# Joining neighbouring VectorE steps in a long-convolution and gated-MLP block

## The chip, the cores and the metric

The kernel runs on one core of a Trainium2 chip. The time is what the device takes for one execution, in microseconds (us); a kernel's time is the median of several executions. Beside the times there is a profile of one execution. It records every instruction on TensorE (PE), its weight loads (PEld), VectorE (DVE), ScalarE (ACT), GpSimd (POOL) and the DMA queue of SyncE (SP). It begins with the first instruction of the program and ends with the last, so its span is a little shorter than the time of the same execution.

## The reference, cut to what matters

```python
mod = (silu(c) @ w_mod).reshape(1, 6, 1, 576)          # sa, ca, ga, sb, cb, gb
h = layernorm(A_q) * (1 + ca) + sa
k_shift[t] = sum(k[t - j] * shift_k[:, j] for j in range(4))      # four taps along the rows
kv = k_shift * v
y  = causal_convolution(kv, ssm_k) + kv * ssm_D        # over 2048 rows, by FFT in float32
x  = A_q + ga * (h * y)
h  = layernorm(x) * (1 + cb) + sb
x  = x + gb * ((silu(h @ w1) * (h @ w3)) @ w2)         # 576 -> 4608 -> 576
```

There are 2048 rows of 576 columns. Inputs and output are bfloat16.

## The kernel before, in words

**The convolution.** It is cut into eight blocks of 256 rows, `s` = 0 to 7, which lie as 128 partitions by two rows of 576. For each block, `kv_rows` (L335) forms kv on VectorE from `kh`, a tile of five shifted rows of k that one DMA fills: a product with tap 0 into `kv` (L345), then for each of three more taps a product into `kvt` (L348) and a sum into `kv` (L349), at last the product with v (L351). `forward` and `forward2` take kv to a spectrum `X` by matmuls (L313, L327); the filter goes the same way to `V`. `pair` (L414) multiplies a spectrum with a filter, 128 by 3456 elements, into `p` (L424) and adds `p` to the accumulator `z` (L426); the first product of a block goes straight to `z` (L419). Block `s` needs s + 1 such pairs. `real_parts` and `inverse` (L557) lead back to rows, `residual` adds them to x, and a layernorm and transposes (`turn_all`, L589, L619) give `h2T`, the left side of the MLP. `p` comes from the pool `prod` and `kv` and `kvt` from `kvp`; each of these tags has one buffer. Older spectra and filters are spilled to memory (`keep_x` L431, `keep_v` L435) and fetched back (L447).

**The MLP.** It works on four row blocks of 512 rows, `r` = 0 to 3. `stream` computes gate and up of one chunk of 128 hidden columns after the other into PSUM (L948, L959), two chunks at a time. `hide` (L963) finishes a chunk: ScalarE writes silu(gate) into `h3` (L967) and copies up into `u` (L969, four buffers), and VectorE multiplies the two in place (L970), 128 by 512 elements. The last row block has `stream_halves` instead (L1009), with the same three steps (L1030, L1032, L1033). `down` (L1042) multiplies `h3` with w2 (L1060) in two halves of 288 columns, over nine steps of four chunks each. Its four accumulators, one for each tile of 128 rows, lie two and two in PSUM tiles; in the last half of the last row block each has a tile of its own (`tail`). At a half's end VectorE multiplies each accumulator with gb (L1077, 128 by 288 from PSUM) and adds it to x (L1078), and SP stores the rows.

**Order.** While row block r streams, the convolution of the two next blocks runs between its chunks: the generator functions yield a cost in microseconds at each step, and `advance` takes as many steps as are due after each chunk. The compiler then orders each engine's queue by what its own model finds ready, and gives out the buffers of a tag in the course of that, so the order in the trace is not the order of the text. Two parts are fixed: in `first_block` (block 0, and the start of block 1) VectorE, ScalarE and TensorE keep the order of the text, and up to the end of the first 24 chunks the SP queue does. In `first_block` a memset of one element of `wm` (L674), put among the steps of `kv_rows(0)`, holds the DMA of the next columns of w_mod (L152) and what SP issues behind it. Weights of the MLP are issued at L899, L900 and L1051.

Of the kernel before, what the change touches and what calls it, by code (L numbers as in the profile page):

```python
# [9 lines left out]
BF16 = mybir.dt.bfloat16  # L10
# [3 lines left out]
ACT = mybir.ActivationFunctionType  # L14

P = 128
S = 2048
D = 576
F = 4608
B = 256  # L20
NBLK = S // B
H = 288
NF = F // P
RB = 512
NRB = S // RB
FC = 4
# [12 lines left out]
def _ap(t, offset, dims):  # L39

    a = t[:]
    return bass.AP(tensor=a.tensor, offset=a.offset + offset, ap=[list(a.ap[0])] + dims)


class _Kernel:
# [289 lines left out]
    def kv_rows(self, s):  # L335

        nc = self.nc
        kh, vt = self.kh, self.vt
        kv = self.kvp.tile([P, 2, D], BF16, name="kv", tag="kv")
        tmp = self.kvp.tile([P, 2, D], BF16, name="kvt", tag="kvt")  # L340

        def tap(j):
            a = self.shk[:, j, :]
            return bass.AP(tensor=a.tensor, offset=a.offset, ap=[list(a.ap[0]), [0, 2], [1, D]])
        nc.vector.tensor_mul(kv[:], kh[:, 3:5, :], tap(0))  # L345
        yield 0.75
        for j in (1, 2, 3):
            nc.vector.tensor_mul(tmp[:], kh[:, 3 - j:5 - j, :], tap(j))  # L348
            nc.vector.tensor_add(kv[:], kv[:], tmp[:])  # L349
            yield 1.5  # L350
        nc.vector.tensor_mul(kv[:], kv[:], vt[:])  # L351
        self.kv = kv
        yield 0.75
# [292 lines left out]
    def first_block(self):  # L646

        nc = self.nc
        since = len(nc.cur_bb.bb.instructions)
        x1 = self.xo[0]  # L650
        self.angles(nc.vector, 1)
        self.whole_turns(1)
        self.waves(1)
        self.shift_taps()
        self.whole_turns(0)

        ps = self.ps()
        nc.tensor.matmul(ps[0:64, 0, 0:5], self.drow[:], self.ident[0:9, 0:9:2], start=True, stop=True)
        nc.tensor.matmul(ps[64:P, 0, 0:4], self.drow[:], self.ident[0:9, 1:9:2], start=True, stop=True)
        nc.scalar.copy(self.dcol[:, 0:4], ps[:, 0, 0:4])  # L660
        nc.scalar.copy(self.dcol[0:64, 4:5], ps[0:64, 0, 4:5])
        tap = self.knat[:, :, 0]
        nc.gpsimd.tensor_add(tap, tap, self.dcol[:])
        self.waves(0)
        self.warm(3, self.h2T[0][:, 0, :])
        sums = [self.small.tile([P, 1], F32, name="l1" + k, tag="sr" + k) for k in "um"]
        self.run_all(self.k_rows(0))
        self.cond_silu()
        self.warm(4, self.h2T[0][:, 0, :])
        rows = self.kv_rows(0)  # L670
        for _ in range(3):
            next(rows)

        nc.vector.memset(self.wm[0:1, 3 * D:3 * D + 1], 0.0)  # L674
        self.load_mod(3, 2)
        self.load_k(1)
        self.run_all(self.w_spectrum(0))
        self.cond()
        self.run_all(rows)
        mean, rstd = self.quick_stats(x1[:, 1, :], "l1")  # L680
        nmr = self.small.tile([P, 1], F32, name="l1nm", tag="nmr1")
        nc.gpsimd.tensor_mul(nmr[:], mean, rstd)
        nc.gpsimd.tensor_single_scalar(nmr[:], nmr[:], -1.0, op=ALU.mult)
        self.run_all(self.x_spectrum(0))
        self.run_all(self.v_block(0))
        self.load_w13(0, 0)
        self.load_kv(1)
        self.load_x(1)
        self.load_w13(1, 1)
        self.load_gb()  # L690
        self.whole_turns(0, True)
        self.waves(0, True)
        X, V = self.X[0], self.V[0]
# [24 lines left out]
        self.normed(0, 0, *st[0])  # L718
        busy = self.shk[:, 0, 0:512]
        self.warm(6, busy)  # L720
        pt = self.turn_split(0)
        self.warm(2, busy)
        self.normed(0, 1, *st[1])
        self.turned_split(pt, 0)
        pt = self.turn_split(1)
        self.warm(3, busy)
        self.turned_split(pt, 1)
        self.accs.pop(0)
        self.hg.pop(0)
        self.start = since  # L730
        return self.in_order(since, [e.engine for e in (nc.vector, nc.scalar, nc.tensor)])[nc.vector.engine]
# [181 lines left out]
    def stream(self, r, jobs, rate, size, finish=False):  # L913
# [5 lines left out]
        nc = self.nc  # L919
        hT = self.h2T[r % 2]  # L920
        items = []
        for job in jobs:
            m = RB // (job[2] - job[1])
            items += [(job, fi, m) for fi in range(0, FC, m)]
        gus, ws = {}, {}
# [37 lines left out]
        def hide(k):  # L963
            (fc, t0, t1, _, _), fi, m = items[k]
            f = fc * FC + fi
            h3 = self.h3[:, f:f + m, t0:t1]
            nc.scalar.activation(h3, gus[k][:, 0, :].rearrange("p (a t) -> p a t", a=m), ACT.Silu)  # L967
            u = self.hp.tile([P, RB], BF16, name="u", tag="u")
            nc.scalar.copy(u[:], gus[k][:, 1, :])  # L969
            nc.vector.tensor_mul(h3, h3, u[:].rearrange("p (a t) -> p a t", a=m))  # L970
            del gus[k]
            self.advance(rate * 2.05)

# [22 lines left out]
    def stream_halves(self, r, jobs):  # L996

        nc = self.nc
        hT = self.h2T[r % 2]
        items = [(job, fi) for job in jobs for fi in range(FC)]  # L1000
        gus, ws = {}, {}
# [25 lines left out]
        def hide(k):  # L1027
            (fc, _, _, _, _), fi = items[k]
            h3 = self.h3[:, fc * FC + fi, :]
            nc.scalar.activation(h3, gus[k][:, 0, :], ACT.Silu)  # L1030
            u = self.hp.tile([P, RB], BF16, name="u", tag="u")
            nc.scalar.copy(u[:], gus.pop(k)[:, 1, :])  # L1032
            nc.vector.tensor_mul(h3, h3, u[:])  # L1033
        begin(0)
        for k in range(len(items)):
            mark = part(k, 0, slice(AHEAD, None))
            begin(k + 1)
            with self.after(mark):
                part(k, 1)
            hide(k)  # L1040

    def down(self, r, rate):  # L1042
        nc = self.nc
        for h in range(2):

            tail = r == NRB - 1 and h == 1
            accs = [self.ps() for _ in range(4 if tail else 2)]
            acc = [accs[t][:, 0, 0:H] if tail else accs[t // 2][:, t % 2, 0:H] for t in range(4)]
            for f0 in range(0, NF, W2C):
# [20 lines left out]
                    for keep, i in leave[2 * h + f0 // (4 * W2C):][0:1]:  # L1070
                        keep(i)
                self.advance(rate * W2C * 4 * 0.126)
            for t in range(4):
                s, cc = 2 * r + t // 2, t % 2
                x1 = self.xo[s]
                g = self.lnp.tile([P, H], BF16, name="og", tag="og", bufs=2)
                nc.vector.tensor_mul(g[:], acc[t], self.gbrow[:, h * H:(h + 1) * H])  # L1077
                nc.vector.tensor_add(x1[:, cc, h * H:(h + 1) * H], x1[:, cc, h * H:(h + 1) * H], g[:])  # L1078
                if r == NRB - 1:
                    rows = self.out[B * s:B * (s + 1), h * H:(h + 1) * H].rearrange("(p c) d -> p c d", c=2)  # L1080
                    nc.sync.dma_start(rows[:, cc, :], x1[:, cc, h * H:(h + 1) * H])
                elif h == 1 and cc == 1:
                    nc.sync.dma_start(self.out[B * s:B * (s + 1), :].rearrange("(p c) d -> p c d", c=2),
                                      x1[:])

    def begin(self, steps, due=0.0):
        self.steps, self.due, self.spent = steps, due, 0.0
# [108 lines left out]
```

## Time and profile before

| what | before |
|---|---|
| median of 5 executions | 521.32 us (519.91 to 523.8) |
| the profiled execution: time, span | 521.21 us, 519.4 us |
| granted TensorE clock, mean | 0.992 |
| instructions | 9194, of them 554 on VectorE |
| moved by DMA | 107.8 MB, 208 GB/s in the mean |

Engine lines give the busy time, its share of the span and the instructions. The rows of slices show the busy share of each fortieth of the span in tenths. A line of a group reads: line, engine, operation, output from inputs, shapes and count, then busy time and the mean duration of one, then the idle time of the engine before them and what ended it. A line of waits reads: who waited for whom, us in total, how often, the longest. A timeline row reads: start, duration, engine, line, operation, and in brackets the idle time before it.

### The profile page before, as it was taken

What the parts mean: (1) busy time and instruction counts of PE and PEld (TensorE: products, weight loads), DVE (VectorE), ACT (ScalarE), POOL (GpSimd) and SP (SyncE); (2) the same over time, 40 slices, a digit from 0 to 9 for tenths busy, and PEclk for the clock granted to TensorE, in tenths of its full rate; (3) what the DMA queues carried; (4) which work ended last, traced back from release to release, by engine and by line L of the source; (5) the groups of instructions that cost most, each with busy time, mean ns of one, the idle gap of its engine ahead of it and who ended that gap; (6) DMA issues with size and microseconds to landing.
All of it is one profiled execution on the core that took longest, in us unless ns stands there. A gap on an engine that the chain in (4) does not pass through costs nothing.

```text
span 519.4 us, 9194 instructions
## 1 busy us (share of the span) xinstructions
PE 497.4 (96%) x3650; PEld 294.7 (57%) x3650; DVE 344.6 (66%) x554; ACT 294.7 (57%) x581; POOL 23.5 (5%) x43
## 2 busy tenths in 40 slices
PE   7999989789989999999899999999999999999996
PEld 3667765357767444344678543433577544444775
DVE  8899898999995364998988996289662212212012
ACT  6668699468343468769427365875806455555000
POOL 3301001000000000000000000000000000000000
PEclk9989999999989999999999999999999999999999
DMA  8947967838978866578989883544455444541462
GB/s 277 326 145 237 300 214 225 267 99 286 322 269 291 283 192 208 176 249 297 261 268 315 319 266 128 192 155 150 145 157 135 141 142 143 173 145 39 122 176 68
DMA packets 102206, 107.80 MB, mean 208 GB/s; under 512 B 5075, under 2 KB 94228, under 8 KB 102164
## 3 DMA queue, kind: packets, MB, share of 16 engines
q1 hardware_dynamic: 102142, 107.21, 65.5%
q8 instruction: 28, 0.46, 0.3%
q14 instruction: 14, 0.11, 0.1%
q10 hardware_dynamic: 22, 0.01, 0.0%
HBM read 96.00 MB, written 11.21 MB: 206 GB/s over the span
## 4 chain that ended last, share of the span: by engine, by line
PE 61%; DVE 22%; ACT 7%; DMA 5%; issue 2%; SPq 2%; POOL 0%; POOLq 0%; ACTq 0%; DVEq 0%
PE ps L948 21%; PE ps L1060 17%; PE ps L1009 14%; DVE p L424 5%; DVE z L426 4%; PE ps L959 3%; ACT junk L454 3%; DVE h L970 2%; DMA knat<-in_A_ssm_k_dram 2%; DVE kv L349 2%; PE ps L327 1%; DMA wst<-in_B_w_dram 1%; DMA V<-Vd 1%; DVE kvt L348 1%; PE ps L313 1%
## 5 line engine op out<-in xcount | busy, mean ns | idle before, releaser
L948 PE MATMUL ps<-h2T,wst 128*128 128x512 bf16 (+1 forms) x1056 | 200.7, 341 | 1.1 <-ACT W L329 0.8
L1060 PE MATMUL ps<-wst,h 128*128 128x288 bf16 x1152 | 147.1, 288 | 4.7 <-DVE og L1077 2.3
L948 PEld LDWEIGHTS <-wst 128*128 128x128 bf16 x1056 | 100.2, 98 | 85.9 <-issue 14.5
L1060 PEld LDWEIGHTS <-h 128*128 128x128 bf16 x1152 | 113.0, 98 | 35.3 <-issue 6.0
L967 ACT ACTIVATE h<-ps 128x512 bf16<-128x512 f32 x108 | 64.8, 600 | 69.2 <-PE ps L959 41.3
L1009 PE MATMUL ps<-h2T,wst 64*128 64x512 bf16 x648 | 70.3, 376 | 0.0
L970 DVE TENSOR_TENSOR h<-h,u 128x512 bf16<-128x512 bf16 x108 | 45.3, 424 | 30.9 <-ACT u L969 30.7
L969 ACT CAST u<-ps 128x512 bf16<-128x512 f32 x108 | 63.2, 585 | 0.0
L424 DVE TENSOR_TENSOR p<-X,V 128x3456 bf16<-128x3456 bf16 x28 | 54.8, 1957 | 2.5 <-DMA X<-Xd 2.3
L426 DVE TENSOR_TENSOR z<-z,p 128x3456 bf16<-128x3456 bf16 x28 | 54.8, 1958 | 0.2
L1009 PEld LDWEIGHTS <-wst 64*128 64x128 bf16 x648 | 31.3, 94 | 38.4 <-DMA wst<-in_B_w_dram 0.4
L1033 DVE TENSOR_TENSOR h<-h,u 128x512 bf16<-128x512 bf16 x36 | 15.3, 425 | 55.2 <-ACT u L1032 55.2
L1030 ACT ACTIVATE h<-ps 128x512 bf16<-128x512 f32 x36 | 21.5, 597 | 36.3 <-PE ps L1009 36.3
L1077 DVE TENSOR_TENSOR og<-ps,gbrow 128x288 bf16<-128x288 f32 x32 | 13.2, 453 | 41.8 <-PE ps L1060 41.8
L454 ACT ACTIVATE junk<-x 128x576 bf16<-128x576 bf16 x54 | 37.0, 686 | 0.5
L959 PE MATMUL ps<-h2T,wst 64*128 64x512 bf16 (+1 forms) x264 | 32.9, 341 | 0.0
L619 ACT ACTIVATE h2T<-ps,sbcol,cbcol 128x256 bf16<-128x256 bf16 x35 | 16.8, 571 | 14.5 <-PE ps L589 14.5
L348 DVE TENSOR_TENSOR kvt<-kh,shk 128x1152 bf16<-128x1152 bf16 x24 | 18.1, 756 | 4.8 <-DMA kh<-in_A_k_dram 4.6
L1032 ACT CAST u<-ps 128x512 bf16<-128x512 f32 x36 | 20.9, 579 | 0.0
L763 ACT CAST y<-ps 128x576 bf16<-128x576 f32 x14 | 8.6, 647 | 20.8 <-PE ps L557 20.8
L959 PEld LDWEIGHTS <-wst 64*128 64x128 bf16 x264 | 8.5, 94 | 21.0 <-issue 20.1
L349 DVE TENSOR_TENSOR kv<-kv,kvt 128x1152 bf16<-128x1152 bf16 x24 | 18.1, 755 | 0.3
(140 smaller groups left out, 389.9 us busy)
## 6 DMA issues: line engine op xcount, KB each, us to landing
wst<-in_B_w_dram SPq DMA_DIRECT2D x80, 512.0 KB, 4.7
wst<-in_B_w_dram SPq DMA_DIRECT2D x72, 288.0 KB, 3.7
X<-Xd SPq DMA_DIRECT2D x8, 864.0 KB, 5.8
Xd<-X SPq DMA_DIRECT2D x6, 864.0 KB, 6.3
wst<-in_B_w_dram SPq DMA_DIRECT2D x80, 64.0 KB, 2.7
kh<-in_A_k_dram SPq DMA_DIRECT2D x7, 720.0 KB, 7.0
Vd<-V SPq DMA_DIRECT2D x4, 864.0 KB, 7.0
V<-Vd SPq DMA_DIRECT2D x4, 864.0 KB, 7.2
```

Of the source, the lines that this page charges most:

```text
L348: nc.vector.tensor_mul(tmp[:], kh[:, 3 - j:5 - j, :], tap(j))
L349: nc.vector.tensor_add(kv[:], kv[:], tmp[:])
L424: nc.vector.tensor_mul(p[:], X[:], V[:])
L426: nc.vector.tensor_add(z[:], z[:], p[:])
L454: self.nc.scalar.activation(junk[:], src[:, i, :], func, scale=scale, accum_out=out[:, col:col + 1])
L948: nc.tensor.matmul(gus[k][:, i, a * n:(a + 1) * n], w[:, 5 * i + ct, (fi + a) * P:(fi + a + 1) * P], hT[:, ct, t0:t1], start=(first and ct ...
L959: nc.tensor.matmul(gus[k][:, i, a * n:(a + 1) * n], w[rows, 4, (fi + a) * P:(fi + a + 1) * P], hT[rows, 4, t0:t1], start=(first and a == 0 ...
L967: nc.scalar.activation(h3, gus[k][:, 0, :].rearrange("p (a t) -> p a t", a=m), ACT.Silu)
L969: nc.scalar.copy(u[:], gus[k][:, 1, :])
L970: nc.vector.tensor_mul(h3, h3, u[:].rearrange("p (a t) -> p a t", a=m))
L1009: nc.tensor.matmul(gus[k][:, i, :], ws[fc][rows, 5 * i + ct if ct < 4 else 4, cols], hT[rows, ct, :], start=swap == 0 and ct == 4, stop=sw ...
L1060: nc.tensor.matmul(acc[t], self.h3[:, f0 + f, t * P:(t + 1) * P], w[:, f, :], start=(f0 + f == 0), stop=(f0 + f == NF - 1))
```

## The change

Three kinds of neighbouring VectorE steps become one instruction each.

- `hide`, in both streams: two chunks share one `u` of twice the size (still four buffers), and one product over 128 by 1024 elements follows the second chunk's copy.
- `kv_rows`: the products with taps 3, 2 and 1 become one instruction of 128 by 3456 elements, the first of the function, written to a tile `p` of the pool `prod`; `kvt` is gone. The product with tap 0, three sums and the product with v follow. The costs that it yields are 2.0 and five times 0.75 where they were 0.75, three times 1.5 and 0.75, and `first_block` takes four steps ahead of the memset in place of three.
- `down`: the two row tiles of one PSUM tile are multiplied and added together, 128 by 576 elements; the last half of the last row block stays as it was, tile by tile. `og` has one buffer of two row tiles, where it had two of one.

```diff
+        p = self.prod.tile([P, 6, D], BF16, name="p", tag="p")
+        nc.vector.tensor_mul(p[:].rearrange("p (j c) d -> p j c d", j=3), _ap(kh, 0, [[D, 3], [D, 2], [1, D]]),
+                             _ap(self.shk, 3 * D, [[-D, 3], [0, 2], [1, D]]))
+        yield 2.0
+        nc.vector.tensor_mul(kv[:], kh[:, 3:5, :], _ap(self.shk, 0, [[0, 2], [1, D]]))
         yield 0.75
-        for j in (1, 2, 3):
-            nc.vector.tensor_mul(tmp[:], kh[:, 3 - j:5 - j, :], tap(j))
-            nc.vector.tensor_add(kv[:], kv[:], tmp[:])
-            yield 1.5
+        for j in range(3):
+            nc.vector.tensor_add(kv[:], kv[:], p[:, 2 * j:2 * j + 2, :])
+            yield 0.75
         nc.vector.tensor_mul(kv[:], kv[:], vt[:])
...
         rows = self.kv_rows(0)
-        for _ in range(3):
+        for _ in range(4):
             next(rows)
...
-            u = self.hp.tile([P, RB], BF16, name="u", tag="u")
-            nc.scalar.copy(u[:], gus[k][:, 1, :])
-            nc.vector.tensor_mul(h3, h3, u[:].rearrange("p (a t) -> p a t", a=m))
+            if k % 2 == 0:
+                self.u = self.hp.tile([P, 2, RB], BF16, name="u", tag="u")
+            nc.scalar.copy(self.u[:, k % 2, :], gus[k][:, 1, :])
+            if k % 2 == 1:
+                h3 = self.h3[:, f - m:f + m, t0:t1]
+                nc.vector.tensor_mul(h3, h3, self.u[:].rearrange("p b (a t) -> p (b a) t", a=m))
...
+                g = self.lnp.tile([P, 2, H], BF16, name="og", tag="og")
+                for cc in ((slice(0, 1), slice(1, 2)) if tail else (slice(0, 2),)):
+                    n = cc.stop - cc.start
+                    ps = acc[2 * a + cc.start].unsqueeze(1) if tail else accs[a][:, :, 0:H]
+                    nc.vector.tensor_mul(g[:, cc, :], ps, _ap(self.gbrow, h * H, [[0, n], [1, H]]))
+                    nc.vector.tensor_add(x1[:, cc, cols], x1[:, cc, cols], g[:, cc, :])
+                    if r == NRB - 1:
+                        nc.sync.dma_start(rows[:, cc, cols], x1[:, cc, cols])
+                    elif h == 1:
+                        nc.sync.dma_start(rows, x1[:])
```

More of the change, by code (lines that the diff above doesn't have):

```diff
@@ L339, in kv_rows @@
         kv = self.kvp.tile([P, 2, D], BF16, name="kv", tag="kv")
[L340 to L345, printed above, removed]
+        p = self.prod.tile([P, 6, D], BF16, name="p", tag="p")
[3 more added lines that the diff above has]
+        nc.vector.tensor_mul(kv[:], kh[:, 3:5, :], _ap(self.shk, 0, [[0, 2], [1, D]]))
         yield 0.75
-        for j in (1, 2, 3):
-            nc.vector.tensor_mul(tmp[:], kh[:, 3 - j:5 - j, :], tap(j))
-            nc.vector.tensor_add(kv[:], kv[:], tmp[:])
-            yield 1.5
+        for j in range(3):
+            nc.vector.tensor_add(kv[:], kv[:], p[:, 2 * j:2 * j + 2, :])
+            yield 0.75
         nc.vector.tensor_mul(kv[:], kv[:], vt[:])
@@ L965, in hide @@
             f = fc * FC + fi
-            h3 = self.h3[:, f:f + m, t0:t1]
-            nc.scalar.activation(h3, gus[k][:, 0, :].rearrange("p (a t) -> p a t", a=m), ACT.Silu)
-            u = self.hp.tile([P, RB], BF16, name="u", tag="u")
-            nc.scalar.copy(u[:], gus[k][:, 1, :])
-            nc.vector.tensor_mul(h3, h3, u[:].rearrange("p (a t) -> p a t", a=m))
+            nc.scalar.activation(self.h3[:, f:f + m, t0:t1], gus[k][:, 0, :].rearrange("p (a t) -> p a t", a=m),
+                                 ACT.Silu)
+            if k % 2 == 0:
[4 more added lines that the diff above has]
+                nc.vector.tensor_mul(h3, h3, self.u[:].rearrange("p b (a t) -> p (b a) t", a=m))
             del gus[k]
@@ L1030, in hide @@
             nc.scalar.activation(h3, gus[k][:, 0, :], ACT.Silu)
-            u = self.hp.tile([P, RB], BF16, name="u", tag="u")
-            nc.scalar.copy(u[:], gus.pop(k)[:, 1, :])
-            nc.vector.tensor_mul(h3, h3, u[:])
+            if k % 2 == 0:
+                self.u = self.hp.tile([P, 2, RB], BF16, name="u", tag="u")
+            nc.scalar.copy(self.u[:, k % 2, :], gus.pop(k)[:, 1, :])
+            if k % 2 == 1:
+                h3 = self.h3[:, fc * FC + fi - 1:fc * FC + fi + 1, :]
+                nc.vector.tensor_mul(h3, h3, self.u[:])
         begin(0)
@@ L1072, in down @@
                 self.advance(rate * W2C * 4 * 0.126)
-            for t in range(4):
-                s, cc = 2 * r + t // 2, t % 2
+            cols = slice(h * H, (h + 1) * H)
+            for a in range(2):
+                s = 2 * r + a
                 x1 = self.xo[s]
[L1076 to L1084, printed above, removed]
+                rows = self.out[B * s:B * (s + 1), :].rearrange("(p c) d -> p c d", c=2)
+                g = self.lnp.tile([P, 2, H], BF16, name="og", tag="og")
[8 more added lines that the diff above has]
+                        nc.sync.dma_start(rows, x1[:])
     def begin(self, steps, due=0.0):
```

## The prediction

> **What bounds the kernel now.** I read the page's busy shares and slices first, then TensorE's waits, the groups by shape, and VectorE's timeline around the waits that bear on it.
>
> ```profile
> PE 497.4 (96%) x3650; PEld 294.7 (57%) x3650; DVE 344.6 (66%) x554; ACT 294.7 (57%) x581; POOL 23.5 (5%) x43
> PE   7999989789989999999899999999999999999996
> DVE  8899898999995364998988996289662212212012
> ```
>
> TensorE has work in 96% of the span, so a faster VectorE can only close TensorE's gaps. VectorE is full in slices 7 to 12 and 17 to 24 (13 us each).
>
> ```profile
> PE ps L557 <- DVE z L543: 2.9, 1, 2.9
> PE ps L1060 <- DVE og L1077: 2.3, 1, 2.3
> PE ps L1060 <- DMA wst<-in_B_w_dram: 1.6, 1, 1.6
> PE ps L378 <- DVE og L1077: 1.0, 1, 1.0
> ```
>
> All of TensorE's gaps sum to 17.8 us; these four, at 100.1, 149.9, 257.4 and 292.2 us, are the ones that hang on VectorE. The third does so indirectly: SP issues the weights behind a spill of X (L431, at 249.43) that waits for VectorE's L365 (ends 249.4).
>
> ```profile
> L424 DVE TENSOR_TENSOR p<-X,V 128x3456 bf16<-128x3456 bf16 x28 | 54.8, 1957 | 2.5 <-DMA X<-Xd 2.3
> L970 DVE TENSOR_TENSOR h<-h,u 128x512 bf16<-128x512 bf16 x108 | 45.3, 424 | 30.9 <-ACT u L969 30.7
> L348 DVE TENSOR_TENSOR kvt<-kh,shk 128x1152 bf16<-128x1152 bf16 x24 | 18.1, 756 | 4.8 <-DMA kh<-in_A_k_dram 4.6
> L1077 DVE TENSOR_TENSOR og<-ps,gbrow 128x288 bf16<-128x288 f32 x32 | 13.2, 453 | 41.8 <-PE ps L1060 41.8
> ```
>
> The last figure ahead of the second bar is the mean ns of one. What an instruction costs its queue is another number, in the timeline's first column (starts):
>
> ```profile
> 91.70 0.42 DVE L970 TENSOR_TENSOR h<-h,u 128x512 bf16<-128x512 bf16 x1
> 92.04 0.75 DVE L531 TENSOR_TENSOR hg<-hg,brow 128x1152 bf16<-128x1152 bf16 x1
> ...
> 135.10 1.96 DVE L424 TENSOR_TENSOR p<-X,V 128x3456 bf16<-128x3456 bf16 x1
> 136.96 0.76 DVE L345 TENSOR_TENSOR kv<-kh,shk 128x1152 bf16<-128x1152 bf16 x1
> 137.63 0.76 DVE L348 TENSOR_TENSOR kvt<-kh,shk 128x1152 bf16<-128x1152 bf16 x1
> 138.43 0.76 DVE L349 TENSOR_TENSOR kv<-kv,kvt 128x1152 bf16<-128x1152 bf16 x1
> ...
> 143.06 1.95 DVE L419 TENSOR_TENSOR z<-X,V 128x3456 bf16<-128x3456 bf16 x1
> 144.93 0.75 DVE L571 TENSOR_TENSOR hg<-hg,y 128x1152 bf16<-128x1152 bf16 x1
> 145.60 1.96 DVE L426 TENSOR_TENSOR z<-z,p 128x3456 bf16<-128x3456 bf16 x1
> ...
> 170.08 0.76 DVE L348 TENSOR_TENSOR kvt<-kh,shk 128x1152 bf16<-128x1152 bf16 x1 [4.60 <-DMA kh<-in_A_k_dram]
> ...
> 193.31 1.95 DVE L424 TENSOR_TENSOR p<-X,V 128x3456 bf16<-128x3456 bf16 x1
> ...
> 208.48 0.76 DVE L345 TENSOR_TENSOR kv<-kh,shk 128x1152 bf16<-128x1152 bf16 x1 [0.20 <-PE ps L327]
> ...
> 209.40 0.75 DVE L349 TENSOR_TENSOR kv<-kv,kvt 128x1152 bf16<-128x1152 bf16 x1
> ```
>
> See three things. The next start comes 0.34 us after a 0.42 us instruction. An instruction that needs the one before it starts later: 137.63 to 138.43 is 0.80, where 136.96 to 137.63 is 0.67. And the compiler's order runs a tap product far ahead of its block: `kvt` is written at 170.08 and read at 209.40.
>
> **The change, part by part.** *Price of an instruction saved.* Durations: (756-424)/640 = 0.519 ns an element, so 424-512x0.519 = 158 ns fixed. Starts (335 ns from an L970 to the next instruction, 667 from an L345, as in the rows at 91.70 and 136.96): (667-335)/640 is the same slope and 335-266 = 69 ns fixed, as neighbours overlap by about 90 ns. Removed: 72 of the 144 `h` products, 2 x 8 in `kv_rows`, 14 + 14 in `down` (the last half, 4 + 4, stays split): 116 of 554. By durations that is 116 x 0.158 = 18.3 us of VectorE, by starts 116 x 0.069 = 8.0. [...]
>
> *silu times up.* Per pair 2 x 0.335 becomes 1024 x 0.519 + 69 = 0.60: 0.07 saved. The first of two products comes one chunk later (about 2 us), and VectorE waits for ACT's `u` once where it did twice. Only `down` reads h3, and the last chunk is finished at the same place as before plus 0.27 us, at least one weight step of 2 us (16 x 0.126) ahead of its use: cost nothing; without that cover 0.27 us a row block. ACT's silu and copies are as before; `u` holds eight chunks where four were held, and no wait for it shows before L969 (idle 0.0).
>
> *kv_rows.* In a chain, 136.96 to 143.06 is 6.10 us; now 1.87 (as L424 to the next start) + 4 x 0.79 + 0.67 = 5.70: 0.40 saved. Interleaved with other work, 8 x 0.668 = 5.34 becomes 1.87 + 5 x 0.668 = 5.21: 0.13. The joined product reads overlapping rows with taps in falling order, which no row shows: at least 0.60 per 1152 as in L424, at most one element a cycle as L1077's slope of 1.04 ns (364 - 64 = 300 ns for 288), 3.6 us. I take the former, since L348 with its repeated tap already costs what L351 does (756, 760). In the first block VectorE ends `kv` at 11.9 in place of 12.3, but X is handed over by ACT at 15.54 and TensorE takes `kv` at 12.45 behind its own work: nothing gained. The memset (L674) that lets SP issue w_mod, knat and weights moves from 9.96 to 10.35; w_mod then lands at 18.5 for a use at 22.4, and the first weights feed L948 at 33: nothing, at most 0.4. The order of SP's and POOL's issues elsewhere is as written before; only `kh` may be released earlier, its load stands in the same place of SP's queue.
>
> *down.* Two products of 0.364 and two sums of 0.217 become 0.67 and 0.37: 1.16 to 1.04. The first result waits for both row tiles (4 x 0.126 = 0.5 us), and PSUM is returned after one product of 0.75 (L564, 576 f32) in place of a second one of 0.45: 0.3 later where VectorE is free. TensorE asks for that bank 8 matmuls (1.0 us) into the next half: covered, 0.2 to spare; else 0.3 a half. One output DMA of two in the second-last half falls away, beside TensorE. In the last half `g` has one buffer: its third product waits for the second sum. Before, sums at 515.42 and 516.12 close the kernel; I count +0.2 (0 to 0.4).
>
> *Sum with the order kept.* In the full stretch 79 to 151.3 lie 24 `h` products (12 x 0.07 = 0.8), one interleaved and one chained `kv_rows` (0.13 + 0.40): 1.3 us, all taken from the 2.3 at 149.9. In row block 1, a wait of 1.6 us for X at 239.5 eats what was saved earlier; behind it 0.3 reaches the gap at 257.4. The 1.0 at 292.2 follows three pair products released by a DMA (280.4): nothing. Row block 3 and TensorE's tail have VectorE idle: nothing. So -1.3 - 0.3 + 0.2 = -1.4. The profiled run took 521.21 (519.4 span + 1.8), the median is 521.32, so no correction: 519.8.
>
> *What the new buffer adds.* `kvt` was private; now the taps sit in `p`, of which there is one, shared with every pair product. The row at 170.08 shows a tap product issued when only kh is there, 38 us before `kv` is free (208.48). If the joined product is placed likewise, `p` stays taken until three sums after 208.5, about 211.5. The pair at 193.31 and its sum (2 x 1.87 = 3.74 us) then move from a stretch where VectorE is half idle (4.9 of 13 us at 196 to 209) into the full one behind it. X's sums at 249.4, the spill, SP's weights and the gap at 257.4 follow: 3.74 less the 0.6 saved there, +3.1. The same stands again at 305.31 (its `kv` at 338.59), with the pair at 313.70: 0 to 3.1 for the inverse at 357, since z has 5 us to spare at 388; I take 1.5. Who waits is thus VectorE's whole queue, behind it TensorE's inverse and SP.
>
> **The rivals.** *1, likeliest: p is held.* -1.3 + 3.1 + 1.5 + 0.2 = +3.5: 524.7 (522.7 to 527.5). For it: 170.08 and 305.31, and a `p` held from 135.10 to 145.60 already. Against: the order is new, and it may give `p` to the pair first. *2, order kept, small gain:* 519.8 (518 to 521). For it: full VectorE ahead of 149.9. Against: it needs the same queue with another buffer. *3, the other side, faster: the held `p` pushes `kv_rows` out of the full stretch.* The 6.1 us at 136.96 wait for the sum at 145.60 and fall behind `og` (151.34), into VectorE's idle time after 157, and the gap at 149.9 closes (2.3). Tap work that goes behind the pairs at 96.05 and 249.62 likewise frees X and z there: the 1.6 at 257.4, and some 0.8 of the 2.9 at 100.1. 521.2 - 4.7 + 0.2 = 516.7. It decides as soon as 2.3 us of work pass `og`. *4, the joined taps run at one element a cycle:* 8 x 1.73 = 13.8 us more VectorE, 3.5 of it before 149.9 and about 1 before 257.4: less 1.6 saved, +3: 524.
>
> **How the numbers follow.** About 0.5% (2.6 us) is what a measurement here can tell from none. Case 1 has 0.42 (0.32 slower, 0.10 within), case 2 0.28 (0.22 within, 0.06 faster), case 3 0.16 (faster), case 4 and other new waits of the reordered queues 0.14 (0.12 slower, 0.02 within). Faster 0.22, same 0.34, slower 0.44. Case 1 gives 524.7; its own range stands above. The range for all reaches from case 3's middle to a bit beyond case 1's end: 516.5 to 528.
>
> **What would show it.** VectorE: 438 instructions, busy near 326 us, but only some 8 us less time from start to start; 690 ns for 128x1024, 1957 for the joined taps. Case 1: a `p` written from kh near 170 and its last sum after 209, no pair between, and a longer gap at 257. Case 2: every pair at its old place, the gap at 149.9 near 1. Case 3: `kv_rows` of block 4 after 151. I am wrong if TensorE's gaps shrink by over 3 us in all, or if the difference lies where VectorE is idle.

## The result, and the profile after

| what | before | changed |
|---|---|---|
| median | 521.42 us (517.95 to 524.85, 79 runs) | 520.62 us (519.03 to 522.37, 44 runs) |
| ratio to before | | 0.998 (95% interval 0.9968 to 0.9993) |
| profiled execution: time, span | 521.21, 519.4 us | 521.62, 519.8 us |
| granted clock, mean | 0.992 | 0.989 |
| VectorE busy, instructions | 344.6 us, 554 | 337.4 us, 438 |
| TensorE idle up to its last matmul | 17.8 us | 14.4 us |

The change brings 0.2%, about 1 us. The interval excludes 1, so the gain is there, but it is small. The busy shares, the slices and the groups of the changed kernel:

```profile
PE 500.7 (96%) x3650; PEld 295.8 (57%) x3650; DVE 337.4 (65%) x438; ACT 293.9 (57%) x581; POOL 23.6 (5%) x43
PE   6999989989999999999997999999999999999996
DVE  8799898998898172998977996189761211211012
L422 DVE TENSOR_TENSOR p<-X,V 128x3456 bf16<-128x3456 bf16 x28 | 54.7, 1955 | 1.8 <-DMA V<-Vd 1.4
L971 DVE TENSOR_TENSOR h<-h,u 128x1024 bf16<-128x1024 bf16 x54 | 37.1, 687 | 22.7 <-ACT u L968 22.7
```

From the groups with shapes apart, the two other joined instructions:

```profile
L341 DVE TENSOR_TENSOR p<-kh,shk 128x3456 bf16<-128x3456 bf16 x8 | 15.6, 1954 | 0.5 <-ACT shk L205 0.4
L1086 DVE TENSOR_TENSOR og<-ps,gbrow 128x576 bf16<-128x576 f32 x14 | 10.6, 756 | 29.2 <-PE ps L1064 28.8
```

Each joined instruction runs at the expected speed; the joined taps are as fast as a pair (1954 ns against 1955). TensorE's waits have changed their names:

```profile
PE ps L587 <- ACT h2row L582: 4.0, 5, 2.2
PE ps L327 <- DVE kv L349: 2.4, 1, 2.4
PE ps L198 <- DMA shk_raw<-in_A_shift_k_dram: 2.2, 1, 2.2
PE ps L376 <- POOL knat L661: 1.3, 1, 1.3
PE ps L1064 <- ACT u L968: 1.0, 1, 1.0
```

The gaps at 100.1 (2.9), 149.9 (2.3), 257.4 (1.6) and 292.2 (1.0) are gone. New are 1.3 us at 6.75 (behind `knat`), 2.4 at 104.8 (behind `kv` of block 3) and 2.2 at 280.2 (behind `h2row`; in it a tile of rows after the second layernorm waits to be transposed). Cut at TensorE's own milestones (the first matmul of each stretch), the two executions compare so:

| stretch, us | before | changed | difference |
|---|---|---|---|
| start to the stream of row block 0 | 33.0 | 33.8 | +0.8 |
| to its down | 94.4 | 93.9 | -0.5 |
| to the stream of row block 1 | 43.2 | 40.5 | -2.7 |
| to its down | 78.2 | 78.9 | +0.7 |
| to the stream of row block 2 | 40.9 | 43.8 | +2.9 |
| to TensorE's end | 225.5 | 224.2 | -1.3 |
| to the span's end | 4.2 | 4.7 | +0.5 |

So little moved in the total because 4.5 us were gained and 4.9 lost in this pair of executions (+0.4 in the profiled times; the medians say -0.8). The experiments take the gains and the losses apart.

**Where block 4's `kv_rows` went.** VectorE's timeline of the changed kernel around 150 us (start, duration, operation):

```profile
146.51 1.95 DVE L422 TENSOR_TENSOR p<-X,V 128x3456 bf16<-128x3456 bf16 x1
148.38 0.75 DVE L1086 TENSOR_TENSOR og<-ps,gbrow 128x576 bf16<-128x576 f32 x1
...
153.11 1.96 DVE L424 TENSOR_TENSOR z<-z,p 128x3456 bf16<-128x3456 bf16 x1
154.98 0.76 DVE L406 TENSOR_TENSOR V<-V 128x1152 bf16<-128x1152 bf16 x1
155.65 1.96 DVE L341 TENSOR_TENSOR p<-kh,shk 128x3456 bf16<-128x3456 bf16 x1
```

The taps come after the pair and after `og`: before, the six microseconds of `kv_rows` lay at 136.96, ahead of it.

**Where the loss at 280 us comes from.** First VectorE, then GpSimd:

```profile
275.18 0.16 DVE L458 TENSOR_TENSOR l2v<-l2s 128x2 f32<-128x2 f32 x1 [0.59 <-ACT junk L452]
276.79 1.96 DVE L422 TENSOR_TENSOR p<-X,V 128x3456 bf16<-128x3456 bf16 x1 [1.45 <-DMA V<-Vd]
278.66 0.15 DVE L460 SCALAR_TENSOR_TENSOR l2v<-l2q,l2v 128x2 f32<-128x2 f32 x1
278.78 1.96 DVE L424 TENSOR_TENSOR z<-z,p 128x3456 bf16<-128x3456 bf16 x1
281.32 0.16 DVE L470 TENSOR_TENSOR l2n<-l2s,l2r 128x2 f32<-128x2 f32 x1 [0.58 <-POOL l2r L464]
```

```profile
278.96 2.32 POOL L464 TENSOR_TENSOR l2r<-l2v,neghalf 128x2 f32<-128x2 f32 x1 [36.37 <-DVE l2v L460]
```

A pair stands in VectorE's queue between the two halves of block 5's second layernorm variance. It waits for a filter from memory (1.45 us) and takes 1.96 us; the power on GpSimd, which needs that variance, then takes 2.32 us beside the sum of 1.96 us. In the kernel before, the variance came first, and the power took 0.69 us:

```profile
278.41 0.16 DVE L460 TENSOR_TENSOR l2v<-l2s 128x2 f32<-128x2 f32 x1
279.22 0.16 DVE L462 SCALAR_TENSOR_TENSOR l2v<-l2q,l2v 128x2 f32<-128x2 f32 x1 [0.65 <-ACT junk L454]
280.25 0.16 DVE L472 TENSOR_TENSOR l2n<-l2s,l2r 128x2 f32<-128x2 f32 x1 [0.87 <-POOL l2r L466]
280.46 1.96 DVE L424 TENSOR_TENSOR p<-X,V 128x3456 bf16<-128x3456 bf16 x1
```

```profile
279.52 0.69 POOL L466 TENSOR_TENSOR l2r<-l2v,neghalf 128x2 f32<-128x2 f32 x1 [33.03 <-DVE l2v L462]
```

The shift (`l2n`), `h2row` and TensorE's transposes follow the power.

### The profile page after: what moved, and what is told of

Its sections match the earlier page's. It is cut to its first block, busy times and chain, and to the rows that moved or that the text cites. A ratio compares the mean times of both kernels' runs of the same rounds, so it can differ in the third digit from the quotient of the medians.

```text
span 519.8 us, 9076 instructions
## 1 busy us (share of the span) xinstructions
PE 500.7 (96%) x3650; PEld 295.8 (57%) x3650; DVE 337.4 (65%) x438; ACT 293.9 (57%) x581; POOL 23.6 (5%) x43
## 4 chain that ended last, share of the span: by engine, by line
PE 66%; DVE 18%; ACT 8%; DMA 3%; issue 2%; POOL 2%; SPq 0%; POOLq 0%; DVEq 0%; ACTq 0%
PE ps L946 20%; PE ps L1064 20%; PE ps L1010 13%; ACT junk L452 3%; PE ps L957 3%; DVE p L422 3%; DVE z L424 2%; PE ps L313 2%; DVE h L971 2%; DVE p L341 2%; DVE kv L347 2%; PE ps L327 2%; PE ps L555 1%; DMA wst<-in_B_w_dram 1%; DMA V<-Vd 1%
## 5 line engine op out<-in xcount | busy, mean ns | idle before, releaser
L422 DVE TENSOR_TENSOR p<-X,V 128x3456 bf16<-128x3456 bf16 x28 | 54.7, 1955 | 1.8 <-DMA V<-Vd 1.4
L424 DVE TENSOR_TENSOR z<-z,p 128x3456 bf16<-128x3456 bf16 x28 | 54.7, 1954 | 0.2
L971 DVE TENSOR_TENSOR h<-h,u 128x1024 bf16<-128x1024 bf16 x54 | 37.1, 687 | 22.7 <-ACT u L968 22.7
L1037 DVE TENSOR_TENSOR h<-h,u 128x1024 bf16<-128x1024 bf16 x18 | 12.5, 692 | 58.1 <-ACT u L1034 58.1
L1086 DVE TENSOR_TENSOR og<-ps,gbrow 128x576 bf16<-128x576 f32 (+1 forms) x18 | 12.3, 689 | 44.1 <-PE ps L1064 43.6
L582 ACT ACTIVATE h2row<-x,l2n,l2r 128x576 bf16<-128x576 bf16 (+1 forms) x24 | 14.0, 663 | 10.5 <-DVE l2n L470 10.5
L347 DVE TENSOR_TENSOR kv<-kv,p 128x1152 bf16<-128x1152 bf16 x24 | 18.1, 756 | 0.3
```

The costliest lines, as they stand in the source:

```text
L347: nc.vector.tensor_add(kv[:], kv[:], p[:, 2 * j:2 * j + 2, :])
L422: nc.vector.tensor_mul(p[:], X[:], V[:])
L424: nc.vector.tensor_add(z[:], z[:], p[:])
L971: nc.vector.tensor_mul(h3, h3, self.u[:].rearrange("p b (a t) -> p (b a) t", a=m))
```

## The experiments

Ratios are to the kernel before, with their 95% intervals; where a difference is given in us, it is that of two ratios times 521.4 us. Most intervals are about 1 us to either side or more, so two rows that differ by less than some 1.5 us (an estimate from the intervals) are not told apart. Two stretches of each profile are set beside them: the start of row block 0's stream, and the time from row block 1's down to row block 2's stream.

| kernel | ratio | idle, us | stream 0 from | down 1 to stream 2 |
|---|---|---|---|---|
| before | 1 | 17.8 | 33.0 | 40.9 |
| changed | 0.998 (0.9968 to 0.9993) | 14.4 | 33.8 | 43.8 |
| p shared, nothing joined | 0.9965 (0.9947 to 0.9983) | 14.2 | 32.0 | 39.2 |
| taps joined alone | 0.9945 (0.9920 to 0.9969) | 13.2 | 34.4 | 40.2 |
| products of down joined alone | 1.0069 (1.0043 to 1.0094) | 19.3 | 33.8 | 42.8 |
| changed, down apart | 0.9916 (0.9896 to 0.9935) | 14.3 | 34.7 | 39.6 |
| changed, down apart, knat on VectorE | 0.9895 (0.9854 to 0.9937) | 13.7 | 32.5 | 39.8 |

**The same kernel again.** A profile is one execution; this one asks which readings belong to the program.

> The changed kernel once more, to see what of its first profile comes back. If the readings describe the program: TensorE idle 14 to 15 us in all, a gap of 2.4 us near 104.8 behind kv, one of 2.2 us near 280.2 behind h2row, no gap over 1 us near 149.9 and 257.4, the sum into knat on GpSimd at 1.6 us, MLP stream of row block 0 from 33.8. If they are accidents of one execution (DMA arrivals): these places and sizes move by a microsecond or more.

Measured: idle 14.8 us, gaps of 2.4 at 104.9 and 1.8 at 279.6, the sum into `knat` again a gap of 1.3 for TensorE, the stream from 33.9. The places stand; a gap of 0.8 at 256.1 is new. Sizes below about 1 us are not to be trusted from one profile.

**The buffer without the joining.**

```diff
-        tmp = self.kvp.tile([P, 2, D], BF16, name="kvt", tag="kvt")
...
         for j in (1, 2, 3):
+            tmp = self.prod.tile([P, 2, D], BF16, name="p", tag="p")
             nc.vector.tensor_mul(tmp[:], kh[:, 3 - j:5 - j, :], tap(j))
```

> The kernel before, with nothing joined; the tap products only take the buffer of the pairs, p, instead of one of their own. Theory A (order): the buffer is given out in the order of the text, so block 4's kv_rows goes behind its pairs by itself, after 150, and the gap at 149.9 (2.3 us) closes with 554 instructions as before; VectorE busy stays near 344 us; TensorE idle falls from 17.8 to about 15; GpSimd's sum into knat stays short and the stream of row block 0 starts at 33.0; time 1 to 2 us under the kernel before. Theory B (fewer instructions give the gain): the gap at 149.9 stays above 1.5 us and the time is that of before or longer.

Theory A holds. With no instruction saved, the ratio is 0.9965 and the gap at 149.9 is gone. The timeline shows the separate products behind the pair and `og`:

```profile
146.43 1.95 DVE L424 TENSOR_TENSOR p<-X,V 128x3456 bf16<-128x3456 bf16 x1
...
155.31 0.75 DVE L348 TENSOR_TENSOR p<-kh,shk 128x1152 bf16<-128x1152 bf16 x1
```

The reason is in how `p` is given out. The text asks for a tile of `p` 36 times; in the changed kernel's trace all 36 writes to `p` come in just that order, though most other instructions do not. For block 4 the text names its pairs with older spectra first, then the taps. A buffer that a tag has only once is handed from user to user in the order of the text, and so the shared tag fixes an order that a private `kvt` had left free.

**The taps alone.** The edit of `kv_rows` and of `first_block` on the kernel before, nothing else.

> The kernel before with only the taps joined (silu times up and the products of down as before). Theory A (order): the gap at 149.9 closes as in the changed kernel, block 4's taps come after 150, and the first block has the same loss (sum into knat 1.6 us, stream of row block 0 from 33.8); time within 0.5 us of the changed kernel, 520 to 521. Theory B (the 72 silu products saved do it): the gap at 149.9 keeps over 1 us and the time is that of before.

0.9945: the gap at 149.9 is closed without 100 of the 116 saved instructions, and the time is about 3 us under before where the changed kernel has 1. It has the first block's loss (a gap of 1.3 at 6.76), but not the one at 280. Theory A is right on the gap and too high on the time: something else in the change costs some 2 us.

**The sum into knat on VectorE.**

```diff
-        nc.gpsimd.tensor_add(tap, tap, self.dcol[:])
+        nc.vector.tensor_add(tap, tap, self.dcol[:])
```

> The changed kernel with one instruction moved: the sum of ssm_D into column 0 of knat runs on VectorE ahead of the joined taps, not on GpSimd beside them. Theory A (GpSimd is held[...]): the transposes of the filter start about 1 us earlier than 8.05, TensorE's gap of 1.3 us at 6.75 shrinks to about 0.3, and the stream of row block 0 starts at 33.0 or before; 0.5 to 1 us under the changed kernel. Theory B (the memset that comes 0.4 us later delays w_mod, and with it the stream): the stream still starts at 33.6 to 33.8, and the time is that of the changed kernel.

In the kernel before, GpSimd's sum of 128x5 elements took 0.25 us. In the changed kernel it takes 1.65, beside VectorE's joined taps (5.96 to 7.92), and TensorE waits for it. Here VectorE does it in 0.18. In this order, before, changed (two rows) and this run (two rows):

```profile
6.79 0.25 POOL L663 TENSOR_TENSOR knat<-knat,dcol 128x5 bf16<-128x5 bf16 x1 [1.53 <-DMA knat<-in_A_ssm_k_dram]
```

```profile
6.35 1.65 POOL L661 TENSOR_TENSOR knat<-knat,dcol 128x5 bf16<-128x5 bf16 x1 [1.09 <-DMA knat<-in_A_ssm_k_dram]
8.05 1.25 PE L376 MATMUL ps<-ident,knat 128*128 128x128 bf16 x10 [1.30 <-POOL knat L661]
```

```profile
6.72 0.18 DVE L661 TENSOR_TENSOR knat<-knat,dcol 128x5 bf16<-128x5 bf16 x1 [1.18 <-DMA knat<-in_A_ssm_k_dram]
6.96 1.25 PE L376 MATMUL ps<-ident,knat 128*128 128x128 bf16 x10 [0.21 <-DVE knat L661]
```

The transposes start at 6.96 (8.05), the gap is 0.21 (1.30), the stream starts at 33.4 (33.8). GpSimd's sum was held beside the taps, as theory A has it; what else the traces show of its condition, two operands in SBUF, stands in the last section. In time, 0.9967 (0.9947 to 0.9987) does not stand clear of the changed kernel's 0.998.

**Block 4's taps ahead of its last pair.**

```diff
                 V = self.old_v(s0 - j, s0)
+                if s0 == 4 and j == 3:
+                    yield from self.kv_rows(s0)
                 yield from self.pair(X, V, s0)
...
-            yield from self.kv_rows(s0)
+            if s0 != 4:
+                yield from self.kv_rows(s0)
```

> The changed kernel with one step moved in the text: kv_rows of block 4 stands ahead of the last pair of its spectra, so that the taps take p before that pair. All instructions stay joined. Theory A (order): the taps are ahead of 151.3 on VectorE again, and if the order is what closed the gap, TensorE waits 1 us or more at 149.9 again (about 1.0 by the prediction's sum for joined instructions in the old order); 0.5 to 1.5 us over the changed kernel. Theory B (instructions saved): no gap over 0.5 us at 149.9 and the time of the changed kernel.

1.0023 (1.0007 to 1.0040), 2.2 us over the changed kernel, yet no gap at 149.9: neither theory said that. The experiment was badly made: at 145.74 the taps (1.95 us) stand where the pair (1.95 us) stood at 146.51, ahead of `og`, and the sums stay behind it. The same length was exchanged, so it does not test what was meant. Why the time grew stays open: the two profiled executions differ by 0.9 us only.

**The variance ahead of the pair.** An order-only dependence on VectorE puts the second sum into block 6 (the pair at 276.79) behind the shift of block 5.

```diff
+        if s == 6 and self.count[s] == 2:
+            self.tc.add_manual_dep(
+                self.newest(), self.l2_last.name,
+                mybir.DependencyInfo(mybir.DependencyClass.NoSync, mybir.DependencyReason.DATA),
+                reason="program order")
```

> The changed kernel with one order fixed on VectorE: the pair that starts at 276.8 goes behind the variance and shift of block 5's second layernorm. Theory A (a pair in front of the variance, and GpSimd's power beside VectorE's sum, hold up h2row): the power takes 0.7 us in place of 2.3, the gaps at 280.2 and 283.1 (2.19 + 0.47) fall below 1 us, the granted clock stays at full in 282 to 286, and row block 2's stream starts at about 288 in place of 290.9; 2 to 4 us under the changed kernel. Theory B (h2row is bound by ACT and by the sums of squares before it): h2row comes at the same time, the gaps stay, no change.

0.9934 (0.9912 to 0.9957), 2.4 us under the changed kernel. The power takes 0.69 us, the gap at 280.2 is gone, row block 2's stream starts at 286.7 (290.9). One pair and one sum moved behind three small instructions bring more than the whole change. Theory A.

**Silu products apart again.** Both `hide` functions as before.

> The changed kernel with the silu products chunk by chunk again (72 more instructions); taps and the products of down stay joined. Theory A (they lie in VectorE's full stretches at 0.07 us a pair, and beside other work elsewhere): VectorE about 5 us more from start to start, the gap at 149.9 at most 0.9 us, time 0 to 1 us over the changed kernel. Theory B (their duration counts, 0.16 us each): 1.5 to 3 us over it.

0.9985 (0.9966 to 1.0005): no difference from the changed kernel can be seen. The 72 instructions, most of those saved, bring nothing that shows; the 0.8 us that the prediction counted for them would lie within the intervals.

**Taps apart again.** `kv_rows` as before, `u` with three buffers for want of space.

> The changed kernel with kv_rows as before (kvt in a buffer of its own, which leaves room for three u tiles of two chunks, not four); silu times up and the products of down stay joined. Theory A (order): the gap at 149.9 is there again, 1.0 to 1.5 us, the one at 104.8 is gone, the first block starts the stream at 33.0; that is case 2 of the prediction: 519.5 to 521. Theory B (the shared p brought nothing): TensorE's idle time as in the changed kernel or less and a time of 519 or less.

1.0133 (1.0100 to 1.0165), far outside what was expected. The old gaps are back (1.49 at 154.2, 1.45 at 259.3), the gap behind `kv` of block 3 is gone and the first block is short (stream from 32.6), as theory A has it. But there are also 4.26 us at 101.9, 1.91 at 41.5 and 2.07 at 285.5 behind `h2row`. The last shows that the loss near 280 does not come with the taps. How much of the rest is due to three `u` tiles is not separated.

**Products of down apart again; and joined alone.** What the runs with the loss at 280 have in common (the changed kernel, and those with silu, taps or knat altered) is the joined `og`.

> The changed kernel with the products of down tile by tile as before; taps and silu products stay joined. The gap behind h2row near 280 is in the three runs with joined og (changed kernel, silu apart, taps apart) and not in the run with joined taps alone. Theory A (the shorter og moves the compiler's order, so that a pair comes ahead of the second layernorm's variance): the variance is ahead of the pairs again, GpSimd's power takes 0.7 us, no gap over 1 us near 280, last out-DMA as before; 2 to 3.5 us under the changed kernel. Theory B (the shared p brings that pair forward): gap and time stay as in the changed kernel.

> The kernel before with only the products of down joined. Theory A (og moves the order at the end of row block 1): a gap of about 2 us behind h2row near 283 and row block 2's stream 2 to 3 us later than in the kernel before, the tail 0.3 longer, the gaps at 149.9 and 257.4 still there; 1 to 3 us over the kernel before. Theory B (as the prediction counted it: 0.12 us saved a half, 0.2 lost at the end): no change.

Apart: 0.9916 (0.9896 to 0.9935), 3.3 us under the changed kernel. Joined alone: 1.0069 (1.0043 to 1.0094), 3.6 us over the kernel before, where 1 to 3 were expected; the gap behind `h2row` is 1.3 us and not 2, and row block 2's stream starts 2.8 us later (292.5 against 289.7). Joined, `og` is a loss, and most of it hangs on an order: the dependence that put the variance ahead of the pair gave 2.4 us of it back. VectorE of the kernel with only `og` joined:

```profile
279.22 0.16 DVE L460 TENSOR_TENSOR l2v<-l2s 128x2 f32<-128x2 f32 x1 [0.54 <-ACT junk L454]
279.90 1.96 DVE L424 TENSOR_TENSOR p<-X,V 128x3456 bf16<-128x3456 bf16 x1 [0.52 <-DMA V<-Vd]
281.78 0.15 DVE L462 SCALAR_TENSOR_TENSOR l2v<-l2q,l2v 128x2 f32<-128x2 f32 x1
```

VectorE and GpSimd of the changed kernel with `og` apart:

```profile
274.17 0.16 DVE L458 TENSOR_TENSOR l2v<-l2s 128x2 f32<-128x2 f32 x1
274.98 0.16 DVE L460 SCALAR_TENSOR_TENSOR l2v<-l2q,l2v 128x2 f32<-128x2 f32 x1 [0.65 <-ACT junk L452]
```

```profile
275.29 0.69 POOL L464 TENSOR_TENSOR l2r<-l2v,neghalf 128x2 f32<-128x2 f32 x1 [33.84 <-DVE l2v L460]
```

With `og` joined, the compiler puts the pair ahead of the second half of the variance, and otherwise behind it, unless the dependence forbids it. Why it does so is open. The joining also took `og` from two buffers to one, and no run has the one without the other. All 17 profiles of this study fall into two groups: the power takes 2.32 or 2.33 us in the nine with joined `og` and no repair, and 0.69 us in the eight others.

**The first block's taps apart.** `kvt` takes the buffer of `y` in block 0.

> The changed kernel with the first block's taps one by one as before (kvt in the buffer of y, which the first block doesn't use); blocks 1 to 7 joined. Theory A (GpSimd's sum into knat waits out the VectorE instruction beside it, 2 us joined, 0.75 apart): the sum takes 0.75 us at most, the transposes start by 7.5, row block 0's stream starts 0.8 to 1.5 us earlier than in the changed kernel (33.8), and the time is lower by as much. Theory B (the start is set by a DMA): no change in either.

The sum takes 0.28 us and the stream starts at 32.7, as theory A says, but the ratio is 0.998 (0.9953 to 1.0006): the time did not fall by the 0.8 to 1.5 us of theory A, as far as this interval tells. Over all profiles, the stream starts at 34.4 in the mean of the eight with the slow sum and at 32.9 in the mean of the nine others, so the 1.5 us at the start are real; that they reach the end is not shown by this run.

**Three repairs together.** The two diffs above, and in the last half `og` of the second tile in the buffer of `y`.

> The changed kernel with three repairs: the sum into knat on VectorE, the pair at 276.8 behind the second layernorm's variance and shift, and in the last half a second buffer (that of y) for og. Theory A (the three losses add): 0.7 + 2.3 + 0.4 us under the changed kernel, about 516.5 to 517.5, TensorE idle near 11 us, span end 4.2 to 4.4 behind TensorE's end. Theory B (a loss repaired early is given back at a later wait): 518 or more.

0.9918 (0.9895 to 0.9942), 3.2 us under the changed kernel, where the three losses sum to 3.4. It cannot be told from the one dependence alone (0.9934), and TensorE's idle time is 14.6 us, not the 11 that theory A said, so this run does not show that the losses add. The span ends 4.2 us behind the last matmul, as in the kernel before (4.7 in the changed one): the single `og` buffer had cost the tail some 0.5.

**A held `p`, built on purpose.**

```diff
         yield from self.mix(self.x_spectrum(s0), beside())
+        if s0 == 4:
+            yield from self.kv_rows(s1)
         yield from self.x_sums(s0)
```

(and not a second time in `others`.)

> The changed kernel with one step moved in the text: kv_rows of block 5 stands ahead of the pair of block 4's new spectrum, so the taps take p early, some 10 us before kv is free, and that pair (at 211 in the changed kernel) has to wait for the third sum. It is what case 1 of the prediction described. Theory A (a held p costs as case 1 said): X's sums and the spill behind them come some 3 us later, a gap of 2 to 5 us at 257 for weights, 2 to 3.5 us over the changed kernel. Theory B (the 3.7 us of pair that wait have slack there, as case 3 said of such moves): block 5's spectrum comes earlier, no new gap over 1 us, within 1 us of the changed kernel.

1.0062 (1.0033 to 1.0091), 4.3 us over the changed kernel. The taps are written at 195.44, 12 us before `kv` is free (207.50), and the pair waits until 215.64 (211.22). That is more than the 2 to 3.5 of theory A, and the place is another: there is no gap at 257. SP issues the fetch of the next filter 3.1 us later than in the changed kernel (273.44 against 270.34), and the pair at 280.14 waits for a filter:

```profile
280.14 1.96 DVE L422 TENSOR_TENSOR p<-X,V 128x3456 bf16<-128x3456 bf16 x1 [3.66 <-DMA V<-Vd]
```

Two pairs now stand ahead of the second half of the variance, `h2row` leaves a gap of 3.7 us, and the granted clock falls to 0.50 behind it (290 to 294).

**Silu joined on top of the shared `p`.**

> The kernel before with the tap products in p (nothing joined there) and the silu products of two chunks joined: what 72 fewer instructions are worth once the order is settled. Theory A (TensorE's remaining gaps behind VectorE are about 4.5 us, and 0.07 us a pair of products is saved): 0 to 1.5 us under the kernel with the shared p alone (0.9965 of the kernel before). Theory B (the later product of the first chunk and one u tile of two chunks cost something): as long as that kernel or longer.

0.9982 (0.9964 to 1.0001), against 0.9965 with the shared `p` alone: no gain, theory B, within what can be told.

**Taps and silu joined, down apart, knat on VectorE.**

> The changed kernel with the products of down tile by tile (as in the version that ran 0.9916 of the kernel before) and, in addition, the sum into knat on VectorE ahead of the taps. Theory A (the first block's loss is a loss of its own): row block 0's stream starts near 33 in place of 34.7, and the time falls 0.7 to 1.5 us further, to about 0.989 to 0.990. Theory B (what starts earlier waits later): 0.9916 again.

0.9895 (0.9854 to 0.9937), 514.78 us in the median: the fastest kernel here, 1.05% under the kernel before and 0.85% under the changed one. The stream starts at 32.5 and idle is 13.7 us. Whether the last 0.2% over the version with `og` apart is real, the intervals leave open.

## Why the prediction was right or wrong, point by point

- **Case 1, "p is held", the likeliest: wrong at its first step.** The row at 170.08 was read as "a tap product is issued when only kh is there". That was true of a private buffer. A tile of a shared tag is given out in the order of the text (36 of 36 writes), and the text names the pairs first. The words before the prediction, that the compiler gives out a tag's buffers in the course of its ordering, had the same error. In the changed kernel, block 5's taps take `p` at 218.25, behind the pairs at 190.91 and 211.22, and no pair waits for them as case 1 had it. The step that failed is the placement; the +3.1 and +1.5 that hung on it did not come. Whether they were sized rightly is not shown: a held `p` built on purpose costs 4.3 us, but not through the gap at 257.
- **Case 3, the pushed `kv_rows`: the mechanism came about.** `kv_rows` of block 4 stands behind `og` at 155.65, and the gaps at 149.9, 257.4 and 100.1 closed. Alone, the shared buffer brings 1.8 us and the joined taps 2.9 us, not 4.7: closing the gap at 100.1 opened one of 2.4 at 104.8, because block 3's taps come behind the same pair.
- **Case 2's number was right by accident.** 519.8 (518 to 521) holds the median of 520.62, but the order was not kept, and the result is a gain of about 4 (the change with `down` apart) and a loss of about 3 (the joined `og`).
- **Price of an instruction.** The shapes came as worked out: 0.60 us from an L971 to the next start, 1.87 for the joined taps, and VectorE's busy time fell by 7.2, close to the 8.0 counted by starts. "Near 326" was a wrong inference: the durations of the groups do add up to some 18 us less (count times mean: 358.3 against 376.6), but the engine's busy line (337.4 against 344.6) counts the overlap of neighbours once. Case 4 took L1077's slope, 1.04 ns an element, for the joined taps (756 ns for L1086's 576 columns against 453 for L1077's 288 give 1.05); they run in 1954 ns, 0.57 an element, which refutes it. Its name, one element a cycle, is the author's: no run shows a cycle of VectorE. For the 72 silu products the sum had 0.8 us in the full stretch; two comparisons show nothing of it, but could not show so little.
- **down: the step that was missed.** "1.16 to 1.04" holds only where the compiler puts another instruction between a product and its sum. Where none stands there, the prediction's own rule for an instruction that needs the one before it applies, 0.79 from start to start in place of 0.67, and the second product comes only after the first sum, which frees the one buffer. First the changed kernel, then the kernel before:

```profile
167.38 0.76 DVE L1086 TENSOR_TENSOR og<-ps,gbrow 128x576 bf16<-128x576 f32 x1 [1.43 <-PE ps L1064]
168.17 0.46 DVE L1087 TENSOR_TENSOR x<-x,og 128x576 bf16<-128x576 bf16 x1
168.73 0.76 DVE L1086 TENSOR_TENSOR og<-ps,gbrow 128x576 bf16<-128x576 f32 x1
```

```profile
170.75 0.82 DVE L1077 TENSOR_TENSOR og<-ps,gbrow 128x288 bf16<-128x288 f32 x2
171.49 0.52 DVE L1078 TENSOR_TENSOR x<-x,og 128x288 bf16<-128x288 bf16 x2
171.92 0.82 DVE L1077 TENSOR_TENSOR og<-ps,gbrow 128x288 bf16<-128x288 f32 x2
```

  From the first product to the third, or to the second joined one, it is 1.35 us where it was 1.17: nothing is saved there. The tail's +0.2 came as +0.5. And the products of down joined alone cost 3.6 us. The prediction looked for a late bank of PSUM; it never asked where the compiler would put the pairs and the variance once `og` was another instruction with another buffer.
- **First block: "nothing, at most 0.4".** It looked at the memset (now at 10.12, not 10.35) and w_mod, and took POOL's queue as unchanged "as written before". The queue is; its instruction's duration is not: it went from 0.25 to 1.65 us, and the stream starts 0.8 us later (1.5 over all profiles).
- **What would have shown it.** Taps of block 4 after 151 was named for case 3, and came. "Wrong if TensorE's gaps shrink by over 3 us" came as well (3.4 in the first profile, 3.0 in the second), while the time hardly moved: TensorE's busy time grew by 3.3 us in their place (500.7 against 497.4), at a mean clock of 0.989 against 0.992.

## What to carry to other kernels

Before counting saved instructions, ask what a new buffer or a shorter instruction does to the order: a tag with one buffer is an order, and here the order was worth 1.8 us with nothing saved, where 72 saved instructions were worth nothing that shows. Take a joint change apart before judging it: one of three parts lost 3.3 us and hid the gain of the others. Small instructions that release another engine (a variance, a power, a sum of five columns) need a fixed place ahead of the long ones.

## What the runs showed of the hardware

**A small GpSimd instruction waited out a long one of VectorE that reads two tiles from SBUF.** The sum into `knat` takes 0.25 to 0.28 us where it meets the end of a VectorE product of 0.75, 0.75 where it meets such a product from its start (the run with `p` shared and nothing joined), and 1.65 beside one of 1.96. The power takes 0.69 us with VectorE idle, 1.07 beside a sum of 0.75 (158.56 in the changed kernel) and 2.32 beside one of 1.96. Each time it ends within 0.6 us of the VectorE instruction's end, and each of these VectorE instructions has both inputs in SBUF. The profile of the kernel before held the warning: its power at 42.24 takes 2.35 us, beside a product of 1.96. An estimate from these times: beside a VectorE instruction 2.6 times as long (1.96 against 0.75), a power that meets its start takes 2.2 times as long (2.32 against 1.07); the prediction did not ask for it.

Beside a VectorE instruction with an input in PSUM, the traces show no such wait. In the changed kernel's first block a power of 128x1 takes 0.56 us at 13.01 with VectorE idle, and 0.55 at 28.44 beside L562's product of 0.75 (from 28.28), which reads `ps`. A product of 128x1 takes 0.19 at 13.65 with VectorE idle, and another 0.19 at 22.29 beside L246's product of 0.75 (from 22.05), which reads `ps` as well. In the kernel before, the product of 13.65 stands at 14.42, beside L408 and L410, which read SBUF alone, and takes 0.41. What holds GpSimd was not tried apart from these times, nor what one input in SBUF alone would do.

**Two microseconds of idle can be followed by little more than half of TensorE's clock, but need not.** In a row of the windows, the last three columns are the granted clock, the DMA share and GB/s. The first rows are the changed kernel behind its gaps of 2.44 us at 104.8 and 2.19 at 280.2; then the same kernel in its second execution, behind the same gap of 2.44 at 104.9:

```profile
108.00:112.00 4.00, 4.00 (x17) 1.98 (x16) 4.00 (x4) 1.93 (x4) 0.00 (x0) 0.57 0.58 184
282.00:286.00 4.00, 3.10 (x19) 2.10 (x20) 3.93 (x3) 3.52 (x8) 0.00 (x0) 0.58 1.04 400
```

```profile
108.00:112.00 4.00, 4.00 (x27) 2.06 (x26) 4.00 (x4) 2.62 (x6) 0.00 (x0) 1.00 0.50 152
```

At 0.57 the window holds 17 matmuls, at 1.00 it holds 27, and from the stream of row block 0 to its down the one execution takes 93.9 us, the other 92.2. A gap of this size thus costs itself, and in one of these two executions, by an estimate from the two stretches, up to 1.7 us more behind it. The kernel before had such a low clock as well, 0.64 in 152 to 156, behind the gap at 149.9; the prediction counted that gap at its own 2.3 us alone.
